# Gate and value of the last two batches: seven block products in place of eight

## Chip, cores and metric

One Trainium2 chip, one core. The metric is the device time of one execution in microseconds (us), a median over runs. The kernel before takes 729.44 us, median of 3 runs (729.43 to 729.71).

## What is computed

Attention with capped scores over 4 batches, 12 heads, 448 positions and 64 dimensions, then a gated MLP on its output (1792 tokens, 768 wide, 1536 hidden), all of it in float32:

```python
scores = cap * np.tanh(scale * np.matmul(q, k.transpose(0, 1, 3, 2)) / cap)
attn = np.exp(scores - np.max(scores, axis=-1, keepdims=True))
attn = attn / (np.sum(attn, axis=-1, keepdims=True) + 1e-09)
x = np.matmul(attn, v)              # heads side by side: 1792 x 768
g = x @ w_gate
h = g * (1.0 / (1.0 + np.exp(-g))) * (x @ w_val)
out = h @ w_out
```

## The kernel before

**Tiling.** A batch is 448 tokens, and everything is kept transposed: a tile has 128 partitions (features) and 448 columns (tokens). A pair is two heads of one batch; a batch has six pairs, whose outputs are the six tiles of `x` (c = 0 to 5). Per pair (`attention(u)`): scores in four parts on TensorE (L345), tanh and exp on ScalarE (L352, L355), the sum over the parts on VectorE (L359), values (L375) and column sums (L383) on TensorE, then reciprocal (L390) and `x` (L394) on VectorE.

**The MLP** (`mlp(k)`) goes in 18 steps per batch: 12 for hidden tiles (first the gate, then the value, of 128 hidden features each), 6 for output tiles. Each step is 36 matmuls of 128x128 weights on 448 columns. Float32 is split in a high part (rounded to float32r, `wh`, `xh`) and a remainder (`wl`, `xl`), and each product of blocks is three matmuls (L510 to L512): high by high, low by high, high by low. So gate and value of one batch are 12 x 36 = 432 matmuls, and of two batches 864. The weights are split anew for each batch: a half step's 128x768 weights come in by DMA (`wf`), are rounded on any of three engines (`wH`, L226, L228, L230) and subtracted on VectorE or GpSimd (`wL`, L235). Batch 0 also narrows the weights from the 64-bit form (L451, L456, L460) and stores them for the others. After the gate comes a tanh (`gt`, L536), then `ga` (L540), `va` (L544), and the split of the hidden tile (`hH`, `hL`); after an output tile a copy out of PSUM (`ov`) and a store.

**Order.** Attention of batch g+1 is spread over the MLP of batch g; the MLP of batch 3 runs with no attention beside it. Every operation is entered in `Plan` with a due time, the engines it may run on and the buffers it takes; `Plan.run` (L92) goes through them and fixes the order of each engine's instructions, which every engine then runs strictly in that order. `BUFS` (L49) says how many buffers each kind of tile has. All of them lie side by side in one SBUF pool, and in one PSUM pool: `sc` 2 x 2 banks, `av` 1, `sm` 1, `mm` 2.

Of the kernel before, what the change touches and what calls it, by code (L numbers as in the profile page):

```python
# [46 lines left out]
LEAD = dict(ld=10, nA=9, st=-1.0, wH=7, wL=4, mlp=0)  # L47

BUFS = dict(  # L49
    rq=2, rk=2, qh=1, ql=1, kh=1, kl=1, rv=2, t=8, s=2, r=2, x32=2, xh=8, xl=8,  # L50
    w64=3, lo=2, wf=7, wh=4, wl=4, th=2, hx=12, o=2, sc=2, av=1, sm=1, mm=2,
)


class Plan:
# [149 lines left out]
def tile_capped_attention_gated_mlp(ctx: ExitStack, tc: tile.TileContext, qd, kd, vd, cap, eye, w1, w2, out):  # L205
    nc = tc.nc
    ENG = {"ACT": nc.scalar, "DVE": nc.vector, "POOL": nc.gpsimd}

    const = ctx.enter_context(tc.tile_pool(name="const", bufs=1))
    dram = ctx.enter_context(tc.tile_pool(name="dram", bufs=1, space=bass.MemoryType.DRAM))  # L210
    pools = ExitStack()
    sb = pools.enter_context(tc.tile_pool(name="sb", bufs=1))
    ps = pools.enter_context(tc.tile_pool(name="ps", bufs=1, space=PSUM))

    def st(shape, dtype, tag):
        return sb.tile(shape, dtype, tag=tag, name=tag, bufs=BUFS[tag])
# [80 lines left out]


    def attention(u):
        g, c = divmod(u, NCC)  # L300
# [415 lines left out]
```

## Time and profile before

| | |
|---|---|
| median of 3 runs | 729.44 us |
| profiled execution, own time | 727.77 us |
| its span, first to last instruction | 725.9 us |
| TensorE busy | 98% of the span |
| VectorE, ScalarE, GpSimd busy | 71%, 44%, 10% |
| granted TensorE clock | 1.00 of full speed in all stages |

The page of the profile names the busy time of each engine, the chain of work that ended last and the costliest groups of instructions. A matmul's end is modelled in this profile (each is listed with some 0.37 us though the next starts 0.20 us later), so for TensorE the starts are read, not the durations. On VectorE too the next instruction can start a little before the one ahead is listed as done.

### The profile page before, as it was taken

The numbers are of one execution on the slowest core, as the hardware profiler recorded it, in microseconds if no ns is written. First come the engines' busy times: TensorE is split into PE (matmuls) and PEld (weight loads), VectorE is DVE, ScalarE is ACT, GpSimd is POOL, SyncE is SP. The second block draws the span as 40 slices with busy tenths as digits, with TensorE's granted clock in tenths as the row PEclk, the third lists the DMA queues.
The fourth block names the chain that finished last, engine by engine and source line by source line (L and its number), as shares of the span: only waits on it lengthen the run. The fifth ranks groups of instructions, "written<-read, shape, count | busy, mean of one in ns | idle before, by whom it ended". The sixth has DMA issues, their size and how long they took to land.

```text
span 725.9 us, 9286 instructions
## 1 busy us (share of the span) xinstructions
PE 708.7 (98%) x3566; PEld 555.5 (77%) x3566; DVE 513.9 (71%) x642; ACT 319.6 (44%) x423; POOL 69.7 (10%) x57
## 2 busy tenths in 40 slices
PE   7889999999999999999999999999999999999996
PEld 2233886777778878778777887787787799999996
DVE  4999998999986658767857467686766546666440
ACT  6989667576772533533522154254344111212100
POOL 1312301112701001101000001011000000000000
PEclk9999999999999999999999999999999999999999
DMA  7555488676797333243244432432322333333310
GB/s 275 207 184 210 164 286 276 232 261 230 254 304 263 123 100 125 66 126 119 73 141 130 148 112 74 148 96 74 121 96 64 116 128 109 109 108 109 101 39 29
DMA packets 42244, 107.64 MB, mean 148 GB/s; under 512 B 4560, under 2 KB 19152, under 8 KB 42192
## 3 DMA queue, kind: packets, MB, share of 16 engines
q1 hardware_dynamic: 41904, 106.74, 44.4%
q8 instruction: 30, 0.49, 0.3%
q10 hardware_dynamic: 288, 0.23, 0.1%
q14 instruction: 22, 0.18, 0.1%
HBM read 87.29 MB, written 19.66 MB: 147 GB/s over the span
## 4 chain that ended last, share of the span: by engine, by line
PE 91%; DVE 3%; ACT 3%; DMA 1%; issue 0%; ACTq 0%
PE mm L510 25%; PE mm L511 24%; PE mm L512 24%; PE av L375 9%; PE sc L345 7%; PE sm L383 2%; ACT t L352 2%; ACT t L355 1%; DVE total L359 1%; DVE r L390 1%; DMA rk<-kd 1%; DVE lo L456 0%; DVE x L394 0%; DVE xl L235 0%; DVE wf L460 0%
## 5 line engine op out<-in xcount | busy, mean ns | idle before, releaser
L510 PE MATMUL mm<-xh,wh 128*128 128x448 f32 x576 | 213.7, 371 | 0.0
L512 PE MATMUL mm<-xl,wh 128*128 128x448 f32 x576 | 210.4, 365 | 0.0
L511 PE MATMUL mm<-xh,wl 128*128 128x448 f32 x576 | 210.4, 365 | 0.0
L235 DVE TENSOR_TENSOR wl<-wf,wh 128x768 fp32r<-128x768 f32 x132 | 125.5, 953 | 2.5 <-ACT wh L226 1.0
L510 PEld LDWEIGHTS mm<-xh,wh 128*128 128x128 f32 x576 | 108.1, 188 | 22.0 <-issue 11.9
L352 ACT ACTIVATE t<-sc 112x896 f32<-112x896 f32 x96 | 83.6, 919 | 81.2 <-PE sc L345 81.1
L512 PEld LDWEIGHTS mm<-xl,wh 128*128 128x128 f32 x576 | 108.2, 188 | 8.7
L511 PEld LDWEIGHTS mm<-xh,wl 128*128 128x128 f32 x576 | 108.2, 188 | 8.2
L510 PE MATMUL mm<-hx,wh 128*128 128x448 f32 x288 | 106.3, 369 | 0.0
L511 PE MATMUL mm<-hx,wl 128*128 128x448 f32 x288 | 105.3, 366 | 0.0
L512 PE MATMUL mm<-hx,wh 128*128 128x448 f32 x288 | 105.3, 366 | 0.0
L226 ACT ACTIVATE wh<-wf 128x768 fp32r<-128x768 f32 x68 | 57.5, 845 | 106.6 <-PE mm L512 87.7
L390 DVE RECIPROCAL r<-sm 128x448 f32<-128x448 f32 x24 | 70.9, 2956 | 42.4 <-PE sm L383 42.1
L230 DVE CAST wh<-wf 128x768 fp32r<-128x768 f32 x62 | 34.7, 559 | 86.5 <-PE mm L512 85.0
L355 ACT ACTIVATE t<-t 112x896 f32<-112x896 f32 x96 | 86.8, 957 | 0.0
L375 PE MATMUL av<-t,rv 112*64 112x448 f32 x384 | 77.5, 545 | 4.5 <-DVE x L394 4.4
L375 PEld LDWEIGHTS av<-t,rv 112*64 112x64 f32 x384 | 25.4, 136 | 48.2 <-issue 38.0
L536 ACT ACTIVATE th<-mm 128x448 f32<-128x448 f32 x48 | 26.2, 545 | 79.8 <-PE mm L512 79.7
L510 PEld LDWEIGHTS mm<-hx,wh 128*128 128x128 f32 x288 | 54.1, 188 | 9.1 <-issue 4.8
L512 PEld LDWEIGHTS mm<-hx,wh 128*128 128x128 f32 x288 | 54.1, 188 | 4.5
L511 PEld LDWEIGHTS mm<-hx,wl 128*128 128x128 f32 x288 | 54.1, 188 | 4.3
L544 DVE SCALAR_TENSOR_TENSOR th<-th,mm 128x448 f32<-128x448 f32 x48 | 29.6, 617 | 38.7 <-PE mm L512 38.6
(62 smaller groups left out, 613.4 us busy)
## 6 DMA issues: line engine op xcount, KB each, us to landing
wf<-w SPq DMA_DIRECT2D x108, 384.0 KB, 3.0
w<-w SPq DMA_DIRECT2D x36, 768.0 KB, 5.2
w<-wf SPq DMA_DIRECT2D x36, 384.0 KB, 3.7
rq<-qd SPq DMA_DIRECT2D x24, 224.0 KB, 3.7
rv<-vd SPq DMA_DIRECT2D x24, 224.0 KB, 2.8
out<-o SPq DMA_DIRECT2D x24, 224.0 KB, 1.9
rk<-kd SPq DMA_DIRECT2D x23, 224.0 KB, 3.7
rk<-kd ACTq DMA_DIRECT2D x1, 224.0 KB, 5.7
```

The source lines that it names most:

```text
L226: nc.scalar.activation(out_, in_, AF.Copy, scale=1.0 if scale is None else scale)
L230: nc.vector.tensor_copy(out_, in_)
L235: ENG[e].tensor_tensor(out_, a, b, op=ALU.subtract)
L345: nc.tensor.matmul(T["sc", u, j][:C, i, :S], lhsT=T[kk, u][r, j * C : j * C + C], rhs=T[qq, u][r], start=n == 0, stop=n == len(z) - 1,)
L352: nc.scalar.activation(T["t", u, j], T["sc", u, j][:C, :, :S], AF.Tanh, scale=icapr)
L355: nc.scalar.activation(T["t", u, j], T["t", u, j], AF.Exp, scale=capr)
L375: nc.tensor.matmul(T["av", u][D * i : D * i + D, :S], lhsT=T["rv", u][:C, i, j * D : j * D + D], rhs=T["t", u, j][:, i], start=j == 0, sto ...
L390: nc.vector.reciprocal(T["r", u], T["sm", u][:, :S])
L510: nc.tensor.matmul(o, lhsT=wh, rhs=xh, start=beg, stop=False)
L511: nc.tensor.matmul(o, lhsT=wl, rhs=xh, start=False, stop=False)
L512: nc.tensor.matmul(o, lhsT=wh, rhs=xl, start=False, stop=fin)
L544: nc.vector.scalar_tensor_tensor(z, z, 0.5, T["mm", k, 1][:, :N], op0=ALU.mult, op1=ALU.mult)
```

## The change

Batches 0 and 1 stay as they were. For batches 2 and 3 together the gate and value are seen, for each hidden tile f, as a 2 by 2 product of blocks: the weights are (gate, value) by (lower, upper half of the 768 inputs), and `x` is (lower, upper half) by (batch 2, batch 3). Written out that is eight block products of 9 matmuls each; Winograd's form needs seven. It takes sums of blocks on both sides:

- Of the weights, for every f: S1 = v_lo + v_hi, S2 = S1 - g_lo, S3 = g_lo - v_lo, S4 = g_hi - S2 (`comb`, 128x384 each). With g_lo, g_hi and v_hi as they are, seven blocks are rounded and split: 3.5 tiles of 128x768 per f, where the two batches before had 4.
- Of `x`, once (`blocks`): T1 to T4 for each of three c, and the split of seven blocks x three c into `X` tiles.
- The products P1, P6, P7, P4 are added in bank `b2`, P2 in `b1`, P5 and P3 in `b3`, in the order P1 P2 P6 P5 P7 P3 P4. Between them partial sums are read: `c1` (P1) before P6, `cu` (P1+P6) before P7, `c5` (P5) before P3, `c22` before P4. `c11`, `c22` and `c12` add a kept copy (`cc`) and a bank on VectorE and give gate of batch 2, value of batch 3, gate of batch 3; `b2` at the end is the value of batch 2.

The output tiles of both batches follow (`outs`), both batches per weight tile, 432 matmuls as before. Since gate and value of batch 2 now wait for attention of batch 3, all 12 pairs of batches 2 and 3 are spread over the MLP of batch 1. The `X` tiles (42 of 128x448) take the memory of attention's tiles: pool `X` opens when pool `A` closes, so the first `X` tile waits for the last use of any tile of attention. In the same way `b1` to `b3` (two banks each) take the PSUM of `sc`, `av`, `sm`, and `cc` the memory of `x`. To fit, `wf` has 5 buffers, not 7, and `xh`, `xl` 7, not 8.

```diff
 BUFS = dict(
-    rq=2, rk=2, qh=1, ql=1, kh=1, kl=1, rv=2, t=8, s=2, r=2, x32=2, xh=8, xl=8,
-    w64=3, lo=2, wf=7, wh=4, wl=4, th=2, hx=12, o=2, sc=2, av=1, sm=1, mm=2,
+    xr=12, X=42, cc=7, hh=6, ss=3, b1=2, b2=2, b3=2,
+    rq=2, rk=2, qh=1, ql=1, kh=1, kl=1, rv=2, t=8, s=2, r=2, x32=2, xh=7, xl=7,
+    w64=3, lo=2, wf=5, wh=4, wl=4, th=2, hx=12, o=2, sc=2, av=1, sm=1, mm=2,
 )
+TAKES = {"X": "A", "R": "W", "C": "R", "win": "att"}
...
+    SHIFT = {"gt": -20.0, "ga": -20.0, "va": -20.0}
...
+        for o in ops.values():
+            for name in {TAKES[POOL_OF[t]] for t, _ in o["alloc"] if POOL_OF[t] in TAKES}:
+                o["deps"] += list(done[name])
...
+            for c in range(2 * NCC):
+                pair_at[2 * NCC + c] = t + L1 + L2 - 4.0 + (72 * mm_us + 7.0 * 12 + 4.0) / (2 * NCC) * c
...
+    PROD = {
+        1: ("b2", 0, 0, "B11"), 2: ("b1", 0, 1, "B21"), 6: ("b2", 1, 1, "T2"), 5: ("b3", 1, 0, "T1"),
+        7: ("b2", 2, 0, "T3"), 3: ("b3", 2, 1, "B22"), 4: ("b2", 3, 0, "T4"),
+    }
...
+        def prod(e, p):
+            bank, n, part, z = PROD[p]
...
+            for c in range(HALF):
+                wh, wl = T["wh", "w", f, n][:, HALF * part + c], T["wl", "w", f, n][:, HALF * part + c]
+                xh, xl = T["xh", z, c], T["xl", z, c]
+                first, end = p in (1, 2, 5) and c == 0, c == HALF - 1
+                nc.tensor.matmul(o, lhsT=wh, rhs=xh, start=first, stop=False, skip_group_check=True)
+                nc.tensor.matmul(o, lhsT=wl, rhs=xh, start=False, stop=False, skip_group_check=True)
+                nc.tensor.matmul(o, lhsT=wh, rhs=xl, start=False, stop=end, skip_group_check=True)
+        before = {6: [("c1", f)], 7: [("cu", f)], 3: [("c5", f)], 4: [("c22", f)]}
...
-    for k in range(18 * NG):
+    for k in range(18 * 2):
         mlp(k)
+    blocks()
+    for f in range(NFC):
+        step(f)
+    for d in range(NDM):
+        outs(d)
```

**How the order moves.** VectorE after the last pair of all, before: the reciprocal and `x` (`x32`) of that pair, then only the split of weights (`wh`, `wl`) until the first `ga` (L540).

```order
L390 RECIPROCAL r_4832<-sm_4821 128x448
L394 TENSOR_TENSOR x32_4848<-av_4812,r_4832 128x448
L235 TENSOR_TENSOR wl_4856<-wf_4617,wh_4846 128x768
L235 TENSOR_TENSOR xl_4866<-x32_4848,xh_4858 128x448
L230 CAST wh_4879<-wf_4629 128x768
L235 TENSOR_TENSOR wl_4881<-wf_4629,wh_4879 128x768
L230 CAST wh_4904<-wf_4651 128x768
L235 TENSOR_TENSOR wl_4906<-wf_4651,wh_4904 128x768
L230 CAST wh_4931<-wf_4695 128x768
L235 TENSOR_TENSOR wl_4933<-wf_4695,wh_4931 128x768
```

All but one (`xl`) of the splits behind that `x` are of weights, two instructions for each half step.

Now, VectorE up to the third block product of the first hidden tile (`X`: split blocks; `xr`: the `x` tiles of batches 2 and 3; `ss`: sums of blocks, of `x` at 128x448 and of weights at 128x384; `wl_4002` serves P1 and P2, `wl_4069` P6 and P5).

```order
L264 TENSOR_TENSOR wl_4002<-wf_3651,wh_3913 128x768
L264 TENSOR_TENSOR X_4008<-ss_3990,X_3994 128x448
L264 TENSOR_TENSOR X_4016<-xr_3429,X_4004 128x448
L264 TENSOR_TENSOR ss_3992<-ss_3992,wf_3651 128x384
L264 TENSOR_TENSOR X_4035<-ss_3969,X_4006 128x448
L259 CAST wh_4040<-ss_3992 128x768
L264 TENSOR_TENSOR ss_4042<-xr_3023,ss_3990 128x448
L264 TENSOR_TENSOR X_4054<-xr_3799,X_4037 128x448
L264 TENSOR_TENSOR ss_4058<-wf_3651,wf_3657 128x384
L264 TENSOR_TENSOR X_4066<-ss_4042,X_4056 128x448
L264 TENSOR_TENSOR ss_4058<-wf_3651,ss_3992 128x384
L264 TENSOR_TENSOR wl_4069<-ss_3992,wh_4040 128x768
```

Between the last `x` and `wl_4069` now stand 39 instructions: 29 on 128x448 tiles with two inputs, four more `wl`, two casts and four sums of weights.

ScalarE at the same place, before: the copies of batch 2's last output tiles (`o`), then the tanh of batch 3's first gate.

```order
L226 ACTIVATE o_4877<-mm_4798 128x448
L226 ACTIVATE o_4929<-mm_4870 128x448
L226 ACTIVATE o_4981<-mm_4922 128x448
L536 ACTIVATE th_5009<-mm_4974 128x448
L226 ACTIVATE wh_5038<-wf_4868 128x768
```

Nothing that a matmul waits for stands close behind those copies.

Now the copy of batch 1's last output tile (`o_4033`) has two casts of blocks behind it; `X_4037` is what `X_4054` above subtracts. `cc_4064` is `c1` of the first hidden tile.

```order
L255 ACTIVATE X_4004<-xr_3429 128x448
L255 ACTIVATE X_4006<-ss_3969 128x448
L255 ACTIVATE o_4033<-mm_3947 128x448
L255 ACTIVATE X_4037<-xr_3799 128x448
L255 ACTIVATE X_4056<-ss_4042 128x448
L255 ACTIVATE cc_4064<-b2_4023 128x448
L255 ACTIVATE wh_4073<-ss_4058 128x768
```

The casts moved in behind a copy that itself waits for the last matmul of batch 1, and on VectorE `X_4054` stands ahead of `wl_4069`.

VectorE in one hidden tile's step, before (batch 3):

```order
L230 CAST wh_5410<-wf_5228 128x768
L540 SCALAR_TENSOR_TENSOR th_5408<-th_5408,mm_5372 128x448
L235 TENSOR_TENSOR wl_5419<-wf_5228,wh_5410 128x768
L544 SCALAR_TENSOR_TENSOR th_5408<-th_5408,mm_5401 128x448
L230 CAST hx_5439<-th_5408 128x448
L235 TENSOR_TENSOR wl_5447<-wf_5256,wh_5437 128x768
L235 TENSOR_TENSOR hx_5439<-th_5408,hx_5439 128x448
```

This is the work for 36 matmuls of one batch.

And now, from `c11` (L477, `b1`) over `c22` (`b2`) and `c12` (`b3`) to `va` (L506):

```order
L477 TENSOR_TENSOR cc_4547<-cc_4547,b1_4537 128x448
L264 TENSOR_TENSOR wl_4568<-wf_4321,wh_4564 128x768
L495 SCALAR_TENSOR_TENSOR th_4566<-th_4566,cc_4547 128x448
L259 CAST wh_4596<-ss_4416 128x768
L264 TENSOR_TENSOR wl_4598<-ss_4416,wh_4596 128x768
L477 TENSOR_TENSOR cc_4594<-cc_4594,b2_4518 128x448
L264 TENSOR_TENSOR ss_4610<-wf_4437,wf_4472 128x384
L264 TENSOR_TENSOR ss_4610<-wf_4437,ss_4532 128x384
L477 TENSOR_TENSOR cc_4580<-cc_4580,b3_4570 128x448
L264 TENSOR_TENSOR wl_4627<-ss_4499,wh_4623 128x768
L506 SCALAR_TENSOR_TENSOR hh_4641<-th_4566,b2_4518 128x448
L495 SCALAR_TENSOR_TENSOR th_4625<-th_4625,cc_4580 128x448
```

One such step stands for two of before (one for each batch). `c11`, `c22`, `c12` and the sums of weights have come in, half a weight tile's split has gone; the sums S1 and S2 are on GpSimd for most f.

## Rows read from the trace of the kernel before

**Rows 1.** The page: busy us of each engine; the chain that ended last, by engine

```profile
PE 708.7 (98%) x3566; PEld 555.5 (77%) x3566; DVE 513.9 (71%) x642; ACT 319.6 (44%) x423; POOL 69.7 (10%) x57
PE 91%; DVE 3%; ACT 3%; DMA 1%; issue 0%; ACTq 0%
```

**Rows 2.** Timeline of PE (start, us): first matmuls of batches 2 and 3, last of all

```profile
414.10 0.36 PE L510 MATMUL mm<-xh,wh 128*128 128x448 f32 x1
...
588.43 0.36 PE L510 MATMUL mm<-xh,wh 128*128 128x448 f32 x1
...
719.55 0.36 PE L512 MATMUL mm<-hx,wh 128*128 128x448 f32 x1
```

**Rows 3.** Stretches: busy us (x) of PE, PEld, DVE, ACT, POOL; clock, DMA

```profile
75.00:165.00 90.00, 90.00 (x439) 69.84 (x437) 84.08 (x102) 58.70 (x79) 15.90 (x12) 1.00 0.71 243
...
414.10:588.40 174.30, 174.30 (x913) 140.52 (x912) 116.60 (x147) 66.82 (x90) 10.56 (x11) 1.00 0.32 103
588.40:675.90 87.50, 87.50 (x433) 81.10 (x433) 52.72 (x82) 16.44 (x24) 0.00 (x0) 1.00 0.34 110
```

**Rows 4.** Groups by line and shape, DVE: count, busy us, mean ns; idle before

```profile
L235 DVE TENSOR_TENSOR wl<-wf,wh 128x768 fp32r<-128x768 f32 x132 | 125.5, 953 | 2.5 <-ACT wh L226 1.0
L359 DVE TENSOR_TENSOR total<-total,t 112x896 f32<-112x896 f32 x46 | 52.2, 1134 | 1.6 <-ACT t L355 1.6
L230 DVE CAST wh<-wf 128x768 fp32r<-128x768 f32 x62 | 34.7, 559 | 86.5 <-PE mm L512 85.0 <-issue 1.5
L235 DVE TENSOR_TENSOR hx<-th,hx 128x448 fp32r<-128x448 f32 x48 | 31.1, 647 | 0.9 <-POOL hx L228 0.9
L540 DVE SCALAR_TENSOR_TENSOR th<-th,mm 128x448 f32<-128x448 f32 x48 | 29.6, 617 | 5.4 <-ACT th L536 4.7
L394 DVE TENSOR_TENSOR x<-av,r 128x448 f32<-128x448 f32 x24 | 14.8, 616 | 0.2
```

**Rows 5.** Timeline of DVE: neighbours that follow without a wait, both widths

```profile
132.41 0.95 DVE L235 TENSOR_TENSOR wl<-wf,wh 128x768 fp32r<-128x768 f32 x1
133.28 0.61 DVE L544 SCALAR_TENSOR_TENSOR th<-th,mm 128x448 f32<-128x448 f32 x1
...
423.03 0.62 DVE L235 TENSOR_TENSOR ql<-rq,qh 128x448 fp32r<-128x448 f32 x1
423.57 0.62 DVE L235 TENSOR_TENSOR kl<-rk,kh 128x448 fp32r<-128x448 f32 x1
```

**Rows 6.** Timelines of PE, DVE, ACT: the last pair's end; the last copy

```profile
566.79 0.93 PE L383 MATMUL sm<-total,ones 113*64 113x448 f32 x4
567.65 0.47 PE L510 MATMUL mm<-hx,wh 128*128 128x448 f32 x1
...
567.77 2.96 DVE L390 RECIPROCAL r<-sm 128x448 f32<-128x448 f32 x1 [3.58 <-PE sm L383]
570.76 0.62 DVE L394 TENSOR_TENSOR x<-av,r 128x448 f32<-128x448 f32 x1
...
571.42 0.58 ACT L226 ACTIVATE xh<-x 128x448 fp32r<-128x448 f32 x1 [0.18 <-DVE x L394]
...
572.17 0.62 DVE L235 TENSOR_TENSOR xl<-x,xh 128x448 fp32r<-128x448 f32 x1
...
720.00 0.54 ACT L226 ACTIVATE o<-mm 128x448 f32<-128x448 f32 x1 [6.75 <-PE mm L512]
```

**Rows 7.** Timelines of POOL and DVE where both work at once

```profile
186.89 7.76 POOL L235 TENSOR_TENSOR ql<-rq,qh 128x448 fp32r<-128x448 f32 x1
...
271.65 1.85 POOL L235 TENSOR_TENSOR wl<-wf,wh 128x768 fp32r<-128x768 f32 x1
...
271.79 1.96 DVE L230 CAST xh<-x 128x448 fp32r<-128x448 f32 x1
...
325.97 1.84 POOL L235 TENSOR_TENSOR wl<-wf,wh 128x768 fp32r<-128x768 f32 x1
...
326.12 0.62 DVE L394 TENSOR_TENSOR x<-av,r 128x448 f32<-128x448 f32 x1
```

More of the change, by code (lines that the diff above doesn't have):

```diff
@@ L210, in tile_capped_attention_gated_mlp, with pool @@
     dram = ctx.enter_context(tc.tile_pool(name="dram", bufs=1, space=bass.MemoryType.DRAM))
-    pools = ExitStack()
-    sb = pools.enter_context(tc.tile_pool(name="sb", bufs=1))
-    ps = pools.enter_context(tc.tile_pool(name="ps", bufs=1, space=PSUM))
+    opened = {}
+    def pool(tag):
+        name = POOL_OF[tag]
+        if name not in opened:
+            if name in TAKES:
+                opened[TAKES[name]][0].close()
+            stack = ExitStack()
+            kind = dict(space=PSUM) if name in ("mm", "att", "win") else {}
+            side = "right" if name in ("W", "R", "C", "att", "win") else "left"
+            opened[name] = stack, stack.enter_context(tc.tile_pool(name=name, bufs=1, side=side, **kind))
+        return opened[name][1]
+    for tag in ("wf", "t", "w64", "mm", "sc"):
+        pool(tag)
     def st(shape, dtype, tag):
-        return sb.tile(shape, dtype, tag=tag, name=tag, bufs=BUFS[tag])
+        return pool(tag).tile(shape, dtype, tag=tag, name=tag, bufs=BUFS[tag])
     def pt(shape, tag):
-        return ps.tile(shape, F32, tag=tag, name=tag, bufs=BUFS[tag])
+        return pool(tag).tile(shape, F32, tag=tag, name=tag, bufs=BUFS[tag])
     plan = Plan(BUFS)
@@ L294, in tile_capped_attention_gated_mlp @@
             for c in range(NCC):
-                pair_at[NCC * (g + 1) + c] = t + 2.0 + PACE * c
-        t += L
+                pair_at[NCC + c] = t + 2.0 + PACE * c
+            for c in range(2 * NCC):
+                pair_at[2 * NCC + c] = t + L1 + L2 - 4.0 + (72 * mm_us + 7.0 * 12 + 4.0) / (2 * NCC) * c
+        else:
+            split_at = t + L1 + 1.0
+        t += L1 + L2
+    win_at = [t + 10.6 * mm_us * f for f in range(NFC)]
+    t += 10.6 * mm_us * NFC
+    out_at = [t + 12 * mm_us * d for d in range(NDM)]
@@ new lines, in blocks, with raw, diff, high @@
+    def blocks():
+        def raw(z, c):
+            return {
+                "B11": ("x32", 2 * NCC + c), "B21": ("x32", 2 * NCC + c + HALF), "B12": ("x32", 3 * NCC + c),
+                "B22": ("x32", 3 * NCC + c + HALF), "T1": ("x32", 3 * NCC + c),
+            }.get(z, (z, c))
+        def diff(e, z, a, b, c):
+            if z != "T1":
+                T[z, c] = st([P, 6 * P], F32, "ss")[:, :S]
+            sub(e, T[raw(z, c)], T[raw(a, c)], T[raw(b, c)])
+        for c in range(HALF):
+            t0 = split_at + 14.0 * c
+            x = [("x", 2 * NCC + c), ("x", 2 * NCC + c + HALF), ("x", 3 * NCC + c), ("x", 3 * NCC + c + HALF)]
+            n = 0
+            for z, a, b, deps in (
+                ("T3", "B22", "B12", x), ("T1", "B12", "B11", x + [("T3", c)]), ("T2", "B22", "T1", [("T1", c)]), ("T4", "B21", "T2", [("T2", c)]),
+            ):
+                users = [("XL", z, c)] + ([("T4", c)] if z == "T2" else [])
+                op((z, c), t0 + n, {"DVE": 0.62, "POOL": 1.3}, lambda e, z=z, a=a, b=b, c=c: diff(e, z, a, b, c), deps,
+                   [("ss", users)] if z != "T1" else [])
+                n += 1.5
+        for n, z in enumerate(BLOCKS):
+            p = next(p for p in PROD if PROD[p][3] == z)
+            for c in range(HALF):
+                def high(e, z=z, c=c):
+                    T["xh", z, c] = st([P, S], F32R, "X")
+                    copy(e, T["xh", z, c], T[raw(z, c)])
+                def low(e, z=z, c=c):
+                    T["xl", z, c] = st([P, S], F32R, "X")
+                    sub(e, T["xl", z, c], T[raw(z, c)], T["xh", z, c])
+                deps = [(z, c)] if z[0] == "T" else [("x", raw(z, c)[1])]
+                order = split_at + 14.0 * c + 1.5 * n
+                fin = [("p", NFC - 1, p)]
+                op(("XH", z, c), order, {"ACT": 0.57, "DVE": 0.39}, high, deps, [("X", fin)])
+                op(("XL", z, c), order + 0.01, {"DVE": 0.62, "POOL": 1.3}, low, [("XH", z, c)], [("X", fin)])
@@ new lines, in outs, with load, wH, wL @@
+    def outs(d):
+        t0 = out_at[d]
+        i = NFC + d
+        for half in range(2):
+            def load(e, half=half):
+                T["wf", "o", d, half] = st([P, 6, P], F32, "wf")
+                nc.sync.dma_start(T["wf", "o", d, half], scratch[i, half])
+            def wH(e, half=half):
+                T["wh", "o", d, half] = st([P, 6, P], F32R, "wh")
+                copy(e, T["wh", "o", d, half], T["wf", "o", d, half])
+            def wL(e, half=half):
+                T["wl", "o", d, half] = st([P, 6, P], F32R, "wl")
+                sub(e, T["wl", "o", d, half], T["wf", "o", d, half], T["wh", "o", d, half])
+            tw = t0 + 3 * mm_us * half
+            fin = [("q", d, 1, 3 * half + 2)]
+            op(("ld", "o", d, half), tw - 24.0, {"SP": 1.09}, load, [("st", i, half)], [("wf", [("wL", "o", d, half)])])
+            op(("wH", "o", d, half), tw - 7.0, {"ACT": 0.85, "DVE": 0.56, "POOL": 0.93}, wH, [("ld", "o", d, half)], [("wh", fin)])
+            op(("wL", "o", d, half), tw - 6.0, {"POOL": 2.04, "DVE": 0.95}, wL, [("wH", "o", d, half)], [("wl", fin)])
+        for b in range(2):
+            for a in range(6):
+                def mm(e, b=b, a=a):
+                    if a == 0:
+                        T["q", d, b] = pt([P, 512], "mm")
+                    o = T["q", d, b][:, :S]
+                    for f in (2 * a, 2 * a + 1):
+                        half, c = divmod(f, 6)
+                        wh, wl = T["wh", "o", d, half][:, c], T["wl", "o", d, half][:, c]
+                        xh, xl = T["hs", f, b]
+                        nc.tensor.matmul(o, lhsT=wh, rhs=xh, start=f == 0, stop=False)
+                        nc.tensor.matmul(o, lhsT=wl, rhs=xh, start=False, stop=False)
+                        nc.tensor.matmul(o, lhsT=wh, rhs=xl, start=False, stop=f == NFC - 1)
+                prev = ("q", d, b, a - 1) if a else ("q", d, 0, 5) if b else ("q", d - 1, 1, 5) if d else ("p", NFC - 1, 4)
+                deps = [prev, ("wL", "o", d, a // 3)] + [("hL", "w", f, b) for f in (2 * a, 2 * a + 1)]
+                op(("q", d, b, a), t0 + (6 * b + a) * mm_us, {"PE": mm_us}, mm, deps, [("mm", [("ov", "o", d, b)])] if a == 0 else [])
+            def ov(e, b=b):
+                T["o", "o", d, b] = st([P, S], F32, "o")
+                copy(e, T["o", "o", d, b], T["q", d, b][:, :S])
+            def ost(e, b=b):
+                nc.sync.dma_start(out[d * P : (d + 1) * P, (2 + b) * S : (3 + b) * S], T["o", "o", d, b])
+            z = t0 + 6 * (b + 1) * mm_us
+            op(("ov", "o", d, b), z, {"ACT": 0.54, "DVE": 0.62}, ov, [("q", d, b, 5)], [("o", [("ost", "o", d, b)])])
+            op(("ost", "o", d, b), z + 0.5, {"SP": 0.7}, ost, [("ov", "o", d, b)])
@@ L592, in tile_capped_attention_gated_mlp @@
             plan.ops[k]["fn"](e)
-    pools.close()
+    for name in ("X", "sb", "C", "mm", "win"):
+        opened[name][0].close()
     large = nc.values_load(
```

142 lines of the change are left out of this document (132 added, 10 removed).

## The prediction, made before the change ran

> **What bounds the kernel now.** First the page: TensorE is busy for 98% of the span and makes up 91% of the chain that ended last [rows 1]. As a matmul's listed time is modelled, I went on to its timeline. The first matmul of batch 3 starts at 588.43, the last of all at 719.55 [rows 2]; between them lie 18 steps of 36, so 647 starts after the first, and 131.12 / 647 = 0.2027 us from start to start. That leaves room for no wait. Batch 2's stage takes 588.43 - 414.10 = 174.33 us [rows 2], 43.2 more than batch 3's, for the six pairs that lie in it: 7.2 us of TensorE for a pair. The stretches then show what the others have left: VectorE is busy for 84.1 of 90 us in batch 0, 116.6 of 174.3 in batch 2 and 52.7 of 87.5 in the gate and value of batch 3, and the clock is 1.00 in all three [rows 3]. So TensorE's own instructions set the time, a matmul taken away is worth 0.2027 us wherever it stood, and a wait put into TensorE's queue is lost for good.
>
> **What goes.** Gate and value of batches 2 and 3 are 864 matmuls; now they are 12 x 7 x 9 = 756. 108 x 0.2027 = **21.9 us** less. Output tiles, attention and batches 0 and 1 have the matmuls that they had. Gone with them are 36 loads and splits of half steps (wl 0.95 us [rows 4]), all beside TensorE's work and worth nothing by themselves.
>
> **What comes, in the steady step of the new stage.** TensorE needs 63 x 0.2027 = 12.8 us for a hidden tile. VectorE has in it three additions from a bank (nearest row: x, 0.62), two ga and two va (0.62 each), three wl at 0.95 and half a one (0.48), a cast (0.56) and two sums of weights (half of a wl, 0.48 each) [rows 4]: 1.9 + 2.5 + 3.3 + 0.6 + 1.0 = 9.3 us, and two remainders more (0.65 each) in the first three tiles. That is hidden, with 2 to 3.5 us to spare; if it were not, each microsecond would count twelvefold. The tight places are the four hand-overs in a step: c1, cu, c5 and c22 each have just one product, 9 x 0.2027 = 1.82 us, to read a bank before TensorE needs it again. The copy of the last output tile starts 720.00 - 719.55 - 0.20 = 0.25 us after its matmuls' turn is over [rows 6]; with 0.62 for the instruction and 0.17 to the next engine (from the cast's end, 571.42 + 0.58, to xl at 572.17 [rows 6]) a hand-over takes 1.04 us. So 0.8 us are spare, and a wl ahead of it that has just begun (0.95) costs 0.15 at most. In the order c22 stands behind a wl whose weights are ready one product earlier, so I put these at nothing; the bound above is 4 x 12 x 0.15 = 7 us.
>
> **What comes once, at the start of the new stage.** X opens only when attention's tiles are done, so every split of x's blocks lies behind the very last x. From the column sums of the last pair TensorE has 12 + 108 matmuls of batch 1's output tiles left, 120 x 0.2027 = 24.3 us, until P1's turn. The reciprocal starts 0.12 after TensorE goes on, and x 2.99 later [rows 6], so 21.2 us before that turn. Then wl_4069, which P6 needs, is the 41st instruction of VectorE with x itself: 30 with two inputs on 448 columns, 5 wl, 4 sums of 384 columns, 2 casts. Neighbours follow each other after 0.54 (448) and 0.87 (768 columns) [rows 5]; half of that for 384. 30 x 0.54 + 5 x 0.87 + 4 x 0.44 + 2 x 0.56 = 23.4 us. P6's turn is 18 x 0.2027 = 3.65 after P1's, so 24.85 after x began: in time, were it the queue alone. But ScalarE holds it up. o_4033 waits for the last matmul of batch 1, starts 0.25 after P1's turn and takes 0.54; X_4037 takes 0.58 (as xh does) and reaches VectorE 0.17 later [rows 6]: X_4054 can start at 1.54. Two more of 448 and two of 384 columns start in 4 x 0.49 = 1.96 us, wl_4069 takes 0.95 and another 0.17 to TensorE: 4.62, against 3.65. **TensorE waits 1.0 us** before P6. Below it is nothing, if ScalarE's neighbours overlap as VectorE's do. Above, with the listed times in place of the starts (30 x 0.62 + 5 x 0.95 + 4 x 0.48 + 1.1 = 26.4) and 2 us of waits for casts, 3.5. I take 1.0, since the chain behind the copy is a wait whatever VectorE does before. P1 itself needs VectorE's queue only up to wl_4002, eleven instructions earlier, and is in time.
>
> **What is moved.** Twelve pairs now lie in batch 1's stage. A pair and a step of gate and value need 7.2 + 7.3 = 14.5 us of TensorE. VectorE needs for them a reciprocal (2.96 [rows 6]), three sums over parts (1.13), x, ql, kl (0.62 each), two wl, ga, va and a remainder [rows 4, 5]: 12.1, and 14.4 if every cast (qh, kh, two wh, hH) fell to it, which other engines share. Tight but under; in batch 0 VectorE at 93% held TensorE up nowhere [rows 3]. The end changes nothing: the hidden tiles' splits wait for X tiles, but these come free product by product in the last step, and in the order no remainder of the first output tile stands behind one that comes later than its matmul. DMA issues on SP move with the pairs; with six pairs beside it, batch 2's stage moved 103 GB/s, and batch 0's steps 243 without holding TensorE up [rows 3].
>
> **The sum.** 727.77 (the profiled execution) - 21.9 + 1.0 = 706.9. The median of the runs is 729.44, 1.67 above that execution, so I expect 708.5.
>
> **The rivals.**
>
> *GpSimd's sums hold the new stage back (slower).* S1 and S2 run on GpSimd for 10 tiles, and P6 and P5 need them. Half of a wl there (1.85 [rows 7]) is 0.9 us each. But one two-input instruction on 448 columns took 7.76 [rows 7], in a stretch of VectorE work without a gap. At that price the two take 15.5 us where TensorE needs 12.8, and 10 x 2.7 = 27 us are added: 735.5, slower than before. It decides from 6.4 us each on, and passes the time of before at 7.4. Against it: in the new stage VectorE has gaps, and its additions from a bank ran beside GpSimd at full speed (x, 0.62, during GpSimd's wl at 325.97), while a cast from SBUF took 1.96 beside one, where casts of nearly twice the width take 0.56 on the mean [rows 4, 7]. 3%.
>
> The Trainium skill ("SBUF — State Buffer", Who interferes with whom) has a rule for this: VectorE and GpSimd share a port pair as an exclusive lock, which a VectorE instruction takes if it has two SBUF inputs or is a copy in a two-port mode, and one with at most one SBUF input does not. The rows above agree, both ways. By that rule wl, the weight sums and the casts lock GpSimd out and are locked out, c11, c22 and c12 are not.
>
> *Hand-overs cost a little each.* If VectorE or ScalarE is behind by one instruction at most of them, 48 x 0.1 to 0.3 us, so 5 to 14: 713 to 723. For it: both engines run strictly in order, and 0.8 us is not much. Against: VectorE has over 2 us spare per step. 9%.
>
> *Five wf buffers slow batch 0, or twelve pairs slow batch 1.* In 90 us of batch 0 VectorE has 5.9 idle [rows 3]. If waits for a wf buffer use that up, TensorE loses what exceeds it: some 2 to 6 us, so 710.5 to 714.5. 13%.
>
> *The matmuls saved are worth nothing*, since something else sets the time: excluded by 0.2027 us throughout.
>
> **How the numbers follow.** The forecast, 707.5 to 711, has 72%; 3% lie below it. The range of 707.0 to 713.5 takes in the forecast's bounds and most of the third rival. A measurement of this kernel can tell some 0.2%, 1.5 us, from no change: faster 0.96, same 0.01, slower 0.03.
>
> **What would show it.** In the changed profile: 756 matmuls into b1 to b3; 12.8 us from one P1 to the next; one gap of about 1 us in TensorE before the first P6, ended by VectorE's wl; weight sums on GpSimd of about 0.9. Wrong would be: steps above 12.8, waits before P7, P3 or P4, or waits in batch 0 or 1.

## The result, and the profile after

The changed kernel takes 708.05 us, median of 4 runs (707.86 to 712.47), against 729.44 before: ratio 0.972, 95% interval 0.9685 to 0.975. Forecast were 708.5. Its executions stand at two levels, 708 and 712 to 713; the profiled one took 712.47 (span 710.7). What sets them apart is a spacing of TensorE's matmuls, told of in the last section; where the level matters below, the rows are of `late_one`, which differs by nine added instructions that cost nothing (below) and whose profiled execution took 707.85. Hidden tiles are counted from 0.

The page of the changed kernel answers to [rows 1]: busy time, then the chain by engine.

```profile
PE 693.1 (98%) x3458; PEld 535.2 (75%) x3458; DVE 535.3 (75%) x659; ACT 363.7 (51%) x506; POOL 94.8 (13%) x83
...
PE 88%; DVE 6%; ACT 3%; DMA 1%; issue 1%; ACTq 0%
```

TensorE is as full as before and still makes up most of the chain: time went because its work did. The waits of TensorE on VectorE in MLP work are two (engine, line, releaser: us in total, times, longest):

```profile
PE mm L797 <- DVE th L827: 1.4, 1, 1.4
...
PE b L458 <- DVE wl L264: 0.2, 1, 0.2
```

The kernel before had neither. There is none ahead of P7, P3 or P4. The stretches answer to [rows 3] (busy us and count of PE, PEld, DVE, ACT, POOL; clock, DMA share, GB/s): batch 0, the rest of attention's time (it ends some 25 us ahead of the new stage), hidden tiles 4 to 11.

```profile
75.00:165.00 90.00, 88.59 (x430) 70.64 (x429) 84.83 (x95) 60.62 (x80) 18.20 (x11) 1.00 0.70 237
165.00:433.50 268.50, 268.50 (x1427) 194.80 (x1425) 212.55 (x243) 150.98 (x195) 31.05 (x28) 1.00 0.46 142
...
510.80:614.90 104.10, 104.10 (x506) 94.55 (x505) 81.37 (x114) 39.22 (x67) 18.76 (x17) 1.00 0.21 65
```

Of these stretches only batch 0 has TensorE not busy throughout; the twelve pairs beside batch 1 (second row) cost no wait, and VectorE has gaps there (212.55 of 268.5). The last matmul answers to [rows 2] best in `late_one` (timeline of PE): the first P1 of hidden tiles 4 and 5, and the last matmul of all.

```profile
509.95 0.36 PE L457 MATMUL b<-X,wh 128*128 128x448 f32 x1
...
522.71 0.36 PE L457 MATMUL b<-X,wh 128*128 128x448 f32 x1
...
699.42 0.37 PE L574 MATMUL mm<-X,wh 128*128 128x448 f32 x1
```

A hidden tile takes 522.71 - 509.95 = 12.76 us, 63 x 0.2025. The last matmul comes 20.13 us earlier than at 719.55 [rows 2]: 21.9 less for 108 matmuls, 2.2 more for the two waits (1.68 and 0.49, below), which leaves 0.4 that these terms don't name. Half of it is there already ahead of the wait in batch 0, where `late_one` runs 0.2 ahead (the same matmul starts at 81.02, before at 81.23).

**The wait before P6.** The timelines of ACT, DVE and PE at the start of the new stage, in the changed kernel:

```profile
458.61 0.54 ACT L255 ACTIVATE o<-mm 128x448 f32<-128x448 f32 x1 [2.62 <-issue]
459.05 0.57 ACT L255 ACTIVATE X<-xr 128x448 fp32r<-128x448 f32 x1
```

```profile
459.65 0.63 DVE L264 TENSOR_TENSOR X<-xr,X 128x448 fp32r<-128x448 f32 x1 [0.79 <-ACT X L255]
...
461.67 0.95 DVE L264 TENSOR_TENSOR wl<-ss,wh 128x768 fp32r<-128x768 f32 x1
```

```profile
458.36 0.37 PE L457 MATMUL b<-X,wh 128*128 128x448 f32 x1
...
462.08 0.37 PE L457 MATMUL b<-X,wh 128*128 128x448 f32 x1
462.67 0.47 PE L458 MATMUL b<-X,wl 128*128 128x448 f32 x1 [0.23 <-DVE wl L264]
462.99 0.36 PE L459 MATMUL b<-X,wh 128*128 128x448 f32 x1
```

The copy starts 0.25 after P1's turn, as worked out, the cast behind it 0.44 later, and the `X` of VectorE that needs the cast 1.29 after P1's turn (1.54 had been worked out). `wl` ends at 462.62, and TensorE starts 0.05 later. P6's first matmul is on time at 462.08: it reads `wh`; only the second reads `wl`. From it to the next lie 0.59 in place of 0.2067, a wait of 0.38, and the matmul behind a wait starts 0.32 later, not 0.21: 0.49 in all.

**The wait in batch 0.** DVE, then POOL, then PE around 80 us in the changed kernel:

```profile
78.89 2.85 DVE L264 TENSOR_TENSOR wl<-wf,wh 128x768 fp32r<-128x768 f32 x1
81.67 2.54 DVE L264 TENSOR_TENSOR hx<-th,hx 128x448 fp32r<-128x448 f32 x1
...
87.00 0.56 DVE L827 SCALAR_TENSOR_TENSOR th<-th,mm 128x448 f32<-128x448 f32 x1
```

```profile
77.89 0.83 POOL L257 TENSOR_SCALAR wh<-wf 128x768 fp32r<-128x768 f32 x1 [8.89 <-DVE lo L743]
78.69 2.24 POOL L644 TENSOR_TENSOR total<-t 112x896 f32<-112x896 f32 x1
81.01 2.72 POOL L644 TENSOR_TENSOR total<-total,t 112x896 f32<-112x896 f32 x1
```

```profile
87.61 0.47 PE L797 MATMUL mm<-xh,wh 128*128 128x448 f32 x1 [1.41 <-DVE th L827]
```

The same instructions in the kernel before, DVE and POOL:

```profile
79.04 0.95 DVE L235 TENSOR_TENSOR wl<-wf,wh 128x768 fp32r<-128x768 f32 x1
79.91 1.31 DVE L235 TENSOR_TENSOR hx<-th,hx 128x448 fp32r<-128x448 f32 x1
...
84.22 0.56 DVE L540 SCALAR_TENSOR_TENSOR th<-th,mm 128x448 f32<-128x448 f32 x1
```

```profile
79.85 0.90 POOL L228 TENSOR_SCALAR wf<-w 128x768 f32<-128x768 f32 x1 [10.69 <-DMA w<-w]
80.71 2.49 POOL L359 TENSOR_TENSOR total<-t 112x896 f32<-112x896 f32 x1
```

VectorE's order is the same; `wl` and `hx` now take 5.39 us and not 2.26, while GpSimd's sums over parts run beside them. GpSimd comes to these 2 us earlier because the planner exchanged what stands before them: the narrowing (`wf<-w`), which waited for its DMA until 79.85, went to ScalarE, and GpSimd casts weights instead (`wh<-wf`, from 77.89). The `ga` (L827) is 2.8 us later, and TensorE, which waits for the bank that it frees, stands for 1.4.

**The additions of the new stage.** DVE, then POOL, by line and shape (count, busy us, mean ns, idle before), answering to [rows 4, 7]:

```profile
L477 DVE TENSOR_TENSOR cc<-cc,b 128x448 f32<-128x448 f32 x36 | 22.3, 619 | 10.9 <-PE b L459 10.8
```

```profile
L413 POOL TENSOR_TENSOR ss<-wf 128x384 f32<-128x384 f32 x10 | 10.6, 1060 | 104.7 <-DVE wl L264 75.8 <-DMA wf<-w 28.9
...
L264 POOL TENSOR_TENSOR ss<-ss,wf 128x384 f32<-128x384 f32 x8 | 10.2, 1276 | 0.6
```

The 36 additions from a bank take 0.62, the sums on GpSimd 1.06 and 1.28 (0.9 had been put). The `ga` of this stage (L495) reads two SBUF tiles, no longer a bank. Where GpSimd is idle it takes 0.62, as from a bank [rows 4]; beside GpSimd's sums it takes longer, and so does a half `wl`. DVE, then POOL, in hidden tile 5 of the changed kernel:

```profile
524.68 1.08 DVE L495 SCALAR_TENSOR_TENSOR th<-th,cc 128x448 f32<-128x448 f32 x1
525.68 1.37 DVE L264 TENSOR_TENSOR wl<-wf,wh 128x384 fp32r<-128x384 f32 x1
...
529.67 0.62 DVE L495 SCALAR_TENSOR_TENSOR th<-th,cc 128x448 f32<-128x448 f32 x1
```

```profile
524.26 1.02 POOL L413 TENSOR_TENSOR ss<-wf 128x384 f32<-128x384 f32 x1 [10.64 <-DVE wl L264]
525.36 1.28 POOL L264 TENSOR_TENSOR ss<-ss,wf 128x384 f32<-128x384 f32 x1
```

So beside GpSimd's sums VectorE loses time in the steady step as well; its spare time hides it.

### The profile page after: what moved, and what is told of

Its sections match the earlier page's. It is cut to its first block, busy times and chain, and to the rows that moved or that the text cites. A ratio compares the mean times of both kernels' runs of the same rounds, so it can differ in the third digit from the quotient of the medians.

```text
span 710.7 us, 9103 instructions
## 1 busy us (share of the span) xinstructions
PE 693.1 (98%) x3458; PEld 535.2 (75%) x3458; DVE 535.3 (75%) x659; ACT 363.7 (51%) x506; POOL 94.8 (13%) x83
## 4 chain that ended last, share of the span: by engine, by line
PE 88%; DVE 6%; ACT 3%; DMA 1%; issue 1%; ACTq 0%
PE mm L797 13%; PE mm L798 12%; PE mm L799 12%; PE av L660 9%; PE sc L630 7%; PE b L458 7%; PE b L459 7%; PE b L457 7%; PE mm L566 4%; PE mm L565 4%; PE mm L564 4%; PE sm L668 2%; DVE total L644 2%; DVE r L675 2%; ACT t L637 1%; ACT t L640 1%
## 5 line engine op out<-in xcount | busy, mean ns | idle before, releaser
L797 PE MATMUL mm<-xh,wh 128*128 128x448 f32 x288 | 108.5, 377 | 1.4 <-DVE th L827 1.4
L798 PE MATMUL mm<-xh,wl 128*128 128x448 f32 x288 | 105.2, 365 | 0.0
L799 PE MATMUL mm<-xl,wh 128*128 128x448 f32 x288 | 105.2, 365 | 0.0
L264 DVE TENSOR_TENSOR wl<-wf,wh 128x768 fp32r<-128x768 f32 (+1 forms) x93 | 94.4, 1019 | 6.5 <-ACT wh L255 4.3
L458 PE MATMUL b<-X,wl 128*128 128x448 f32 x252 | 92.8, 368 | 0.2 <-DVE wl L264 0.2
L457 PE MATMUL b<-X,wh 128*128 128x448 f32 x252 | 92.7, 368 | 0.0
L459 PE MATMUL b<-X,wh 128*128 128x448 f32 x252 | 92.7, 368 | 0.0
L255 ACT ACTIVATE wh<-wf 128x768 fp32r<-128x768 f32 (+1 forms) x70 | 55.6, 794 | 46.8 <-PE mm L799 11.6
L799 PEld LDWEIGHTS mm<-xl,wh 128*128 128x128 f32 x288 | 54.1, 188 | 4.4
L798 PEld LDWEIGHTS mm<-xh,wl 128*128 128x128 f32 x288 | 54.1, 188 | 3.8
L797 PE MATMUL mm<-hx,wh 128*128 128x448 f32 x144 | 53.7, 373 | 0.0
L799 PE MATMUL mm<-hx,wh 128*128 128x448 f32 x144 | 52.7, 366 | 0.0
```

The lines of the kernel that those rows point to most:

```text
L457: nc.tensor.matmul(o, lhsT=wh, rhs=xh, start=first, stop=False, skip_group_check=True)
L458: nc.tensor.matmul(o, lhsT=wl, rhs=xh, start=False, stop=False, skip_group_check=True)
L459: nc.tensor.matmul(o, lhsT=wh, rhs=xl, start=False, stop=end, skip_group_check=True)
L797: nc.tensor.matmul(o, lhsT=wh, rhs=xh, start=beg, stop=False)
L798: nc.tensor.matmul(o, lhsT=wl, rhs=xh, start=False, stop=False)
L799: nc.tensor.matmul(o, lhsT=wh, rhs=xl, start=False, stop=fin)
```

## The experiments

Two theories stood at the start: the saved matmuls count in full, less the two waits above; or part of the gain is hidden elsewhere (hand-overs, GpSimd's sums, buffers). Each run makes one edit; where it adds or confines instructions, the planner's order moves with it, which is told where it matters.

**The same kernel once more** (`again`).

> The changed kernel once more, unaltered. In its profiled execution TensorE's matmuls start 0.2067 us apart from about 434 us to the end, where they start 0.2027 apart in most of the kernel before; that execution took 712.47, three of the others 707.9 to 708.2. If the wider spacing belongs to single executions, the median stays at 708.0 +- 0.5, and a profile taken in a shorter execution has 0.2027 in the stage of the seven products (12.77 us from one first product to the next) and lasts 4 to 5 us less. If it belongs to the change (block products or the later output tiles run at 0.2067 always), this profile has 13.02 us per hidden tile again.

Measured: 710.26, median of 6 runs, from 707.83 to 713.03: 707.83, 708.03, 708.19 and 712.33, 712.52, 713.03. Two levels, half and half, nothing between, so the median is not the 708.0 expected. The profile was again taken in an execution of the upper level (712.33) and shows 13.02 us per tile; this run alone does not decide whether the spacing belongs to the change. `early_wl` and `late_one` do: profiled at the lower level, they show 12.77 for the same products.

**An eighth product** (`eighth`): nine more matmuls per hidden tile, into a bank that nothing reads.

```diff
+            if p == 4:
+                if f == 0:
+                    T["eighth"] = pt([P, 512], "mm")
+                for c in range(HALF):
...
+                    nc.tensor.matmul(o, lhsT=wh, rhs=xh, start=c == 0, stop=False)
+                    nc.tensor.matmul(o, lhsT=wl, rhs=xh, start=False, stop=False)
+                    nc.tensor.matmul(o, lhsT=wh, rhs=xl, start=False, stop=c == HALF - 1)
```

> The changed kernel with nine more matmuls behind P4 in each hidden tile, into a bank that nobody reads: as many matmuls as eight block products have, all sums and hand-overs as in the change. My theory: TensorE's count alone sets the time of this stage, so 108 x 0.2027 = 21.9 us come back: 729.9, and 14.6 us from one first product to the next. Rival: the stage of seven products is held by something else too (hand-overs, VectorE), so that nine matmuls fill what was a wait: 715 to 727.

Measured: 729.99, median of 10 runs (nine from 729.59 to 730.12, one at 734.92), ratio 1.001 (0.9996 to 1.003) to the kernel before. That is 22.1 over the 707.9 of the changed kernel's lower level, for 108 x 0.2027 = 21.9, and its trace has 14.59 us from one P1 to the next: the whole gain is the number of matmuls.

**The kernel before with the smaller buffers** (`before_wf5`): `wf` 5, `xh` and `xl` 7, nothing else.

> The kernel before with 5 wf buffers and 7 each of xh and xl, the cuts that the change made for memory, and nothing else. If these cuts bring the wait at 87.6 us in batch 0 (a late VectorE beside GpSimd's sums), TensorE waits there in this kernel too and it takes 0.5 to 2 us more than before: 730 to 731.5. Rival: that wait comes from the other edits of the change (the due times of gt, ga and va moved ahead by 20): the time stays at 729.5.

Measured: 730.63, ratio 1.0019 (1.0009 to 1.0028). Its wait of TensorE in batch 0:

```profile
PE mm L510 <- DVE th L540: 1.4, 1, 1.4
```

It is there, 1.4 long at the same place, behind the same 2.85 and 2.55 us of VectorE, without any block product. So it comes from the buffers, through the order that the planner made of them; which of the two cuts does it, `wf` or `xh` and `xl`, was not taken apart. (A second wait, 0.8 at 189.7, is not in the changed kernel.)

**The two waits taken away one by one** (`early_ga`: the reciprocal behind the gate that is late; `early_wl`: the split that P6 needs ahead of three others; `both_moves`).

```diff
+    shift(("rec", 6), ("ga", 1))
...
+    shift(("wL", "w", 0, 1), ("T4", 2))
```

> One instruction moved: on VectorE in batch 0 the reciprocal of the seventh pair comes after the ga of the second hidden tile, not before it. My theory: of the two waits that the changed kernel added, the one at 87.6 us (1.41) is that ga, which stood behind a reciprocal on a VectorE that ran late because two instructions beside GpSimd's sums took 2.85 and 2.54 us. Expected: this wait goes and 1.4 us with it, 706.6; the profile has no gap of TensorE before 90 us. Rival: the matmuls wait for the weights of the third step, or the wait comes back at the next instruction of the late VectorE; then 707.5 to 708.1.

> One instruction moved: on VectorE the remainder wl for the third block product (P6) of the first hidden tile comes before the remainders of the last two blocks of x, whose casts stand behind a copy on ScalarE. My theory: the wait before the second matmul of the first P6 (0.39 us more than the usual spacing) is that chain and nothing else. Expected: the gap goes, 0.4 us less: 707.6. Rival: c1, which must wait for the moved remainder of x, holds P6 instead: 0 to +0.5, 708.0 to 708.5.

> Both moves together. If the two waits are independent and are all that the change lost, 1.4 + 0.4 = 1.8 us less than the changed kernel: 706.2, and no gap of TensorE is left but those of the kernel before. Rival: a wait taken away early comes back later, as VectorE is late anyway: 706.6 to 708.

Measured, medians with the lowest run: 707.05 (706.96), 707.6 (707.44), 707.14 (706.92; ratio 0.971, 0.9688 to 0.9732). The wait before P6 goes as worked out, 0.4. In batch 0 the lowest run falls by 0.9 and not 1.4: the next gate waits in its stead, by 0.4. So `early_ga` and `both_moves` miss their figures (706.6 and 706.2): a wait came back, as their rivals said, in `early_ga` by less than the 707.5 named.

**That one, too** (`three_moves`): `both_moves` and

```diff
+    shift(("wL", 3, 1), ("ga", 2))
```

> Both moves, and in batch 0 the split of half a step's weights (the one behind which the third gate waited at 93.8) put behind that gate. Theory: the gate can start 0.1 after its tanh, at 93.0, and TensorE's gap of 0.73 at 94.4 goes, 0.4 to 0.5 us less than with both moves: lowest 706.4 to 706.5, if nothing else waits for the split. Rival: the split is late in its turn and the gap only moves on by a few matmuls, 706.9 as with both moves. Either way some executions stand 4 to 5 us higher, with the wider spacing of matmuls that the executions before showed.

Measured: 706.3, median of 5 (705.96 to 710.85), ratio 0.9695 (0.9673 to 0.9717). The lowest is 0.4 under the figure expected. No wait is left in gate, value or output tiles; lowest against lowest it is 1.9 us under the changed kernel, the best version of this study. Its two levels stay (705.96 to 706.3, and 710.41, 710.85).

**All sums of weights on GpSimd** (`sums_gpsimd`).

```diff
-            op(key("S", n), t0 - 12.0 + n * 1.2, {"DVE": 0.52, "POOL": 1.1}, ...
+            op(key("S", n), t0 - 12.0 + n * 1.2, {"POOL": 1.1}, ...
```

> All four sums of weights of each hidden tile on GpSimd, where it has about two: the suspected cost doubled. GpSimd took 1.06 us for one such sum in the changed kernel; four are 4.2 of 12.8 us. My theory: no change (708.0 +- 0.4), as VectorE has 3 us of idle time in a step to make good what it loses beside GpSimd. Rival: the lock between the two engines makes wl and casts late, waits appear in most steps: +0.2 per step or more, 710.5 to 716.

Measured: 709.17 (708.79 to 709.25), ratio 0.9725 (0.9707 to 0.9743). Some 1.1 us over the lower level, where no change was expected. Its last matmul stands 0.7 later than in `late_one`, all of it from the start of the stage; 0.3 more lie behind the last matmul. Its waits on `wl` in the new stage:

```profile
PE b L458 <- DVE wl L264: 0.7, 2, 0.4
```

No step waits later. The rival with GpSimd's sums needed 6.4 us for each; they take 1.01 to 1.72 here. An addition from a bank beside such a sum keeps its 0.62 (DVE, POOL):

```profile
507.22 0.62 DVE L477 TENSOR_TENSOR cc<-cc,b 128x448 f32<-128x448 f32 x1 [0.27 <-PE b L459]
```

```profile
507.02 1.01 POOL L264 TENSOR_TENSOR ss<-wf 128x384 f32<-128x384 f32 x1 [4.14 <-DVE wl L264]
```

**One more VectorE instruction ahead of c11, c22 and c12** (`pads_one`): 128x448, two SBUF inputs, its result read by nothing, in every hidden tile.

```diff
+        for i, p in ((2, 2), (5, 7), (6, 3)):
+            op(("pad", f, p, 0), t0 + i * dt - 0.1, {"DVE": 0.62}, pad, [("p", f, p)])
```

> One more instruction of VectorE (two inputs, 128x448, a result that nobody reads) right ahead of each of c11, c22 and c12, in every hidden tile: each such hand-over is later by 0.54 us, and VectorE has 1.6 us more per step. My theory: a hand-over takes about 0.9 of the 1.82 us that it has, and VectorE some 9.3 of 12.8, so the time stays: 708.0 +- 0.5. Rival: hand-overs have less room than that, and each step waits: 12 x 0.3 or more, over 711.

Measured: 714.75 (712.98 to 715.53), ratio 0.980 (0.9772 to 0.9824). The expectation fell. Waits of TensorE, and stretches early in the stage:

```profile
PE b L457 <- DVE cc L477: 3.9, 3, 3.0
```

```profile
466.00:484.00 18.00, 16.98 (x83) 15.07 (x81) 17.95 (x26) 7.80 (x13) 9.42 (x5) 1.00 0.21 63
...
486.10:490.50 4.40, 4.36 (x14) 3.90 (x15) 3.30 (x6) 1.69 (x3) 1.32 (x1) 0.62 0.00 0
```

In the first two tiles VectorE is busy for 17.95 of 18 us, beside 9.42 of GpSimd's, to which the planner gave more sums (16.44 and 4.44 in the changed kernel). After the wait of 3.0 that ends at 486.1 the granted clock is 0.62 on the mean for 4.4 us. Two readings stood open: the hand-overs are tight everywhere, or only the first tiles have no room. This trace speaks for the second: tiles 3 to 10 take 12.76 to 12.77 each without a wait, and the listed waits are in tiles 1, 2 and 11. To test it, the next runs leave the first three tiles alone.

**One, and two, ahead of c22 in tiles 3 to 11** (`late_one`, `late_two`).

```diff
+        pads = [("pad", f, n) for n in range(1)] if f >= 3 else []
...
-        op(("c22", f), t0 + 5 * dt, {"DVE": 0.62}, lambda e: plus(2, "b2"), [("p", f, 7), ("c5", f)])
+        op(("c22", f), t0 + 5 * dt, {"DVE": 0.62}, lambda e: plus(2, "b2"), [("p", f, 7), ("c5", f)] + pads)
```

> One added VectorE instruction of 128x448 right ahead of c22, in hidden tiles 3 to 11 alone; its result is read by nothing. Theory 1 (hand-overs have cover once the stage runs, and the run with one more instruction at three places lost its time in the first tiles): in the traces c22 starts 0.48 after the last matmul of P7 starts, ends 0.62 later, and P4's turn is 2.03 after that matmul, so 0.88 us are spare with 0.05 for the way to TensorE; 0.54 more leaves 0.34. No wait in tiles 3 to 11, 12.77 us per tile, time as without it (lowest 707.8). Theory 2 (the hand-overs themselves are what that run paid for, 7 us over 36 added instructions): 9 x 0.2, so 709.6.

> Two such instructions ahead of c22 in tiles 3 to 11. Theory 1: 1.08 us more against 0.88 spare, so TensorE waits 0.20 us ahead of P4 in each of 9 tiles, ended by c22, and nowhere else: 12.97 us per tile, 1.8 us in all, 709.6. Theory 2: 9 x 0.4 and more, above 711.4.

`late_one`: 707.81 at the lowest, 709.64 the median of 6 (three at each level); no wait in any hidden tile but the one before P6. The hand-over has room for an instruction in each steady tile, and `pads_one` paid for the first tiles and, 0.5 us, for the last. `late_two`: 718.56 (718.4 to 718.75), far over the first theory's 709.6, and over the 711.4 from which the second began. It waits eight times ahead of P4, 1.3 in seven tiles (from 508.01 to 509.51 in the first of them, with 0.20 due), and not at all in tile 10. PE, DVE and POOL in the first of them, and the added instruction in this and the next tile (shortest, median, longest ns):

```profile
509.51 0.47 PE L457 MATMUL b<-X,wh 128*128 128x448 f32 x1 [1.13 <-DVE cc L477]
```

```profile
506.82 2.10 DVE L264 TENSOR_TENSOR pad<-X 128x448 f32<-128x448 f32 x2
```

```profile
506.46 1.32 POOL L264 TENSOR_TENSOR ss<-wf,ss 128x384 f32<-128x384 f32 x1 [6.44 <-DVE wl L264]
```

```profile
L264 DVE TENSOR_TENSOR pad<-X x4: 625/1032/1439, 506.8 to 522.5; 128x448 f32<-128x448 f32 x4
```

Seeing VectorE fuller, the planner had put S4 on GpSimd, just there, and S3 ahead of the added two (as ahead of the one in `late_one`). The first of them takes 1.44 beside S4. That asks for a run with S4 elsewhere.

**The same, S4 back on VectorE** (`late_two_dve`).

```diff
+            order.pop(next(n for n, y in enumerate(order) if y[0] == ("S", "w", f + 2, 4)))
+            order.insert(next(n for n, y in enumerate(order) if y[0] == ("c22", f)) + 1, (("S", "w", f + 2, 4), "DVE"))
```

> As the run with two added instructions ahead of c22, but S4 of tiles 5 to 11 goes back from GpSimd, where the planner had put it in that run, to VectorE, behind c22. That run waited 1.30 us ahead of P4 in seven tiles; in each the first added instruction took 1.44 us on VectorE beside S4's 1.32 on GpSimd, where it takes 0.62 with GpSimd idle. Theory (the two engines lock each other out of SBUF for two-input instructions): without GpSimd's sum there the added instruction takes 0.62 again, the wait falls by 0.82 to 0.48 or less, seven times, and 0.35 stays in tile 11: lowest 711.1 or somewhat under, against 718.4. Rival (VectorE's queue alone): S4 on VectorE adds 0.5 per tile to a queue that is late already, the waits stay at 1.3 or grow, 718 or above.

Measured: 712.4 (712.24 to 713.2), 6.2 us less at the lowest, though VectorE has more to do. The added instructions, and TensorE ahead of P4:

```profile
L264 DVE TENSOR_TENSOR pad<-X x4: 617/622/625, 506.7 to 520.7; 128x448 f32<-128x448 f32 x4
```

```profile
507.89 0.37 PE L459 MATMUL b<-X,wh 128*128 128x448 f32 x1
508.57 0.47 PE L457 MATMUL b<-X,wh 128*128 128x448 f32 x1 [0.31 <-DVE cc L477]
508.88 0.37 PE L458 MATMUL b<-X,wl 128*128 128x448 f32 x1
```

0.62 each, and the wait is 508.57 - 507.89 - 0.20 = 0.48, the figure expected: two added instructions put `c22` back by 1.08 and S3 ahead of them by 0.27, against the 0.88 spare. So a sum of 1.3 us on GpSimd held VectorE up by 0.82, and this is shown with the sum alone moved. Of the 1.1 by which the lowest run lies over the 711.1 expected, 0.8 is the step behind each wait (508.57 to 508.88, 0.31 and not 0.20), eight times.

## Why the prediction was right, point by point

- **What goes, 21.9.** Shown: `eighth` gives back 22.1, and a hidden tile takes 12.76 where 12.8 were put. The 13.02 of the profiled execution, a sign of being wrong by the prediction's own list ("steps above 12.8"), is 63 x 0.2067 without a wait. One count was off, without effect: 36 loads are gone, but only 24 of 144 whole splits of weights, and 12 half ones have come in.
- **The steady step.** Right that it is hidden. VectorE is busy for 10.2 us of a steady tile (81.37 over the eight from 4 to 11), where 9.3 were put: `ga` and a half `wl` run beside GpSimd's sums and take 1.08 and 1.37, not 0.62 and 0.48. `late_one` shows room for one more instruction ahead of c22. The estimate of a hand-over was too dear: c22 ends 1.10 after the last matmul of P7 starts, so 0.90 after its turn is over, and from there to TensorE it took 0.05, not 0.17: 0.95 for 1.04. "2 to 3.5 us to spare" misled for the first tiles: with late splits of `x` VectorE is busy for 12.46 of 13.51 us in tile 0 and 11.68 of 13.02 in tile 1, and `pads_one` shows the rest used up.
- **Once, 1.0 before P6.** The chain was right, its size off: 0.49. The wait is one matmul later than put, as P6's first reads only `wh`; ScalarE's neighbours start 0.44 apart, not 0.54; and the way to TensorE is 0.05.
- **Twelve pairs beside batch 1.** Right, no wait.
- **Five `wf` buffers.** Put at nothing in the sum and at 13% as a rival; it happened, at 1.68 us (2 to 6 had been named), by another way than the rival said. VectorE's 5.9 us of idle time was not used up by waits for a buffer. The planner, short of buffers, gave a narrowing to another engine, GpSimd's sums moved 2 us and came to lie beside two-input VectorE work. `before_wf5` shows that the buffers are the cause, `early_ga` and `three_moves` the place; that GpSimd's sums are what slows VectorE there is read from the rows, and shown by a run only for the sum in `late_two`.
- **The sum.** Against the profiled execution of before, 727.77 - 21.9 + 0.5 + 1.7 = 708.1; measured at the lower level 707.85. The sum on record had 1.2 too little for waits, and then added 1.67 for what the median of before lay over its profiled execution, for which the changed kernel's lower level shows nothing. The two nearly cancel: 708.5 stands closer to 708.05 than its terms deserve. Where the 1.67 of the kernel before comes from stays open, since no execution of it at 729.4 was profiled. There is luck in the median, too: three of four executions stood at the lower level, in `again` three of six, and the upper one, at 712 to 713, lies outside the forecast of 707.5 to 711. The prediction had no term for that.
- **GpSimd's sums as the bound.** Did not happen; it had been given 3%. But the lock that the Trainium skill states ("SBUF — State Buffer", Who interferes with whom) fits the wait in batch 0 and the larger part of those in `late_two`: the runs agree with it, by 2.85 in place of 0.95 for `wl` in batch 0 and 1.44 in place of 0.62 for the added instruction, and additions from a bank beside such sums keep their 0.62 (`sums_gpsimd`). The wait before P6 has another cause, the copy in ScalarE's queue.

## What to carry to other kernels

Where TensorE has no gap, fewer matmuls are worth their full spacing, as long as the other engines have room for the additions that buy them and read each bank before the next product on it. After a cut of buffers look at the order of GpSimd beside a busy VectorE: sums there that moved by 2 us cost TensorE 1.7 here. Room of a mean step tells nothing of the first steps of a stage; look at the wait list and the busy share there separately.

## What the hardware showed that was not expected

**Two spacings at one clock.** Matmuls of the same shape follow each other after 0.2027 or 0.2067 us, 2% apart, both with a granted clock of 1.00. From P1 to P1 a tile takes 12.76 in `late_one` and 13.02 in the changed kernel's profiled execution (PE, first P1 of tiles 2 and 4):

```profile
484.89 0.37 PE L457 MATMUL b<-X,wh 128*128 128x448 f32 x1
...
510.93 0.37 PE L457 MATMUL b<-X,wh 128*128 128x448 f32 x1
```

(510.93 - 484.89) / 126 = 0.2067. In every profiled execution of the changed kernel and its variants a long stretch of the wider spacing begins at about 433, where attention's last matmuls hand over to batch 1's last output tiles. In most it ends near 461 to 471 (`late_one`, `early_ga`, `early_wl` among them), in four it lasts to the end: the profiled execution of the change, `again`, `both_moves`, `three_moves`. From 461 to the end are some 1170 matmuls, x 0.0040 = 4.7 us, about the distance of the two levels. The spacing changed at waits or near them, but the same wait before P6 ended it in one execution and not in another; in `early_wl` it ended with no wait that the profile lists. Shorter stretches of it stand elsewhere, in the kernel before too (some 95 matmuls from 220 to 240 us); the 1.67 us by which that kernel's median lies over its profiled execution would be some 420 more such matmuls, an estimate that no trace confirms. What decides is open, and no kernel was made for it alone.

**The clock after a wait.** In `pads_one` (PE):

```profile
488.13 0.57 PE L458 MATMUL b<-X,wl 128*128 128x448 f32 x1
488.51 0.57 PE L459 MATMUL b<-X,wh 128*128 128x448 f32 x1
...
490.65 0.36 PE L459 MATMUL b<-X,wh 128*128 128x448 f32 x1
490.86 0.37 PE L457 MATMUL b<-X,wh 128*128 128x448 f32 x1
```

The matmuls behind the wait of 3.0 us are 0.20 apart at first, then 0.37 for some 3 us, the lower of the clock's two levels (1.2 GHz, for 2.4), and 0.21 again from 490.65. After the waits of 1.1 to 1.4 in `late_two` (509.5) and in batch 0 (87.6) the spacing does not grow, and the clock stays at 1.00.
